# A longer SyncE time for k's turning transfer in the planner of an attention and soft-MoE kernel, with a new order of the attention

## The chip, the cores and the metric

The kernel runs on one core of a Trainium2 chip. The metric is the device time of one execution in microseconds (us). A kernel's time is the median of several executions.

## What is computed

Three layers follow each other. The reference, cut to its core:

```python
# attention: q, k, v are (4, 12, 448, 64)
q_n, k_n = rmsnorm(q, g_q), rmsnorm(k, g_k)
attn = softmax(scale * q_n @ k_n.T)
x = attn @ v                               # -> (1792, 768)
# soft mixture of experts, 8 experts with 4 slots each
logits = x @ phi
slot_input = softmax(logits, axis=0).T @ x
slot_out[e] = relu(slot_input[e] @ w1[e]) @ w2[e]
x = softmax(logits, axis=1) @ slot_out
# one more feed-forward layer
h = x @ w_in
out = (h * sigmoid(1.702 * h)) @ w_out
```

## The kernel before

The attention takes two heads at a time: 24 pairs, numbered p = 0 to 23. Two pairs (four heads) share one load of q, k and v. For each pair the steps are these.

- **Preparation.** `square` and `meansq` (L412, L417), the inverse root (`invert`, L434 to L448), `gain` (L465), `qn` and `kn` (L472). Then q and k are each split into two float16 halves: `qhi` and `khi` on ScalarE (L476, L479), `qlo` (L482) and `klo` (L487). `k2` and `q2` copy the high halves once more (L288 on ScalarE, L290 elsewhere).
- **Turning.** A DMA transpose issued by SyncE (L499) turns the rows so that the head's dimension lies along the partitions: `tka` for k (16 blocks of 128x128), `tqa` for q (8 blocks) and, later, `tqb` for q's second form (8 blocks). Pairs 0 and 1 are turned on TensorE instead. The buffer that `tka` reads exists once (`ka=1`), so `khi` of the next pair has to wait until `tka` has landed.
- **Row maxima.** Four steps `mx` on TensorE (L529) make a first, rough score. Each has a `max` on VectorE (L534). The PSUM tile between them exists once (`mx=1`), so `mx` number g+1 waits for `max` number g. The maxima go into q's second form, which `tqb` turns.
- **Scores.** Seven steps `sc` on TensorE (L545) with seven `exp` on ScalarE (L549), four `pv` steps (L559, L564), partial sums `esum` (L552), the sums' turns, and the output's turn `x` (L610, L611) with its scaling `xmul` (L623, L627).

No order is written out by hand. `op()` records each step with its engine, an estimated duration, a due time and what it needs. `run()` replays them: at each point it takes the engine whose next step can start first, and among the steps of that engine that can start then the one with the smallest due time. The steps are issued in that order, and each engine works through its own row strictly in order. Two tables steer it: `ON` says for each pair which engine does a step (D = VectorE, P = GpSimd, A = ScalarE), and `SHIFT` is added to the due time of each kind of step.

SyncE's row holds all of the attention's loads (`lq`, `lk`, `v`: L386 to L400), the turning transfers, and the first expert weights: `early` (L115, L124) and, near the end, `e0` to `e3` and `ev`, which go into buffers that the attention has given up. A step of SyncE has two prices in the planner. The duration in `op()` is how long SyncE itself is taken, and `QUEUE` says when the transfer will have landed; `QUEUE` counts 3.0 for `tka` and 1.5 for `tqa` and `tqb`.

Where TensorE would stand idle, the planner puts in small matmuls on the identity (`warm`, L380), which compute nothing that is used.

After the attention come the soft-MoE stage (to about 410 us), which streams the expert weights, and the last layer, in which TensorE works without a pause.

Of the kernel before, what the change touches and what calls it, by code (L numbers as in the profile page):

```python
# [20 lines left out]
def soft_moe_block_kernel(  # L21
# [30 lines left out]
    T = 8.862  # L52

    ON = dict(
        gain="PDPDPDDDPDDPDPDPDDPDDDDD",
        qn="DPPDPPPPPPDPPPDPPPPPDPDD",
        kn="DPDDDPPPPPDDPPDPPPDDPDPP",
        qlo="PPDPPPDPDDPPDDPPDPDDPPPD",
        klo="DDDDDDPPPDPDDPDDDPDPDPDD",
        q2="PPDAAADAPDDDDDAAAAPDPPDA",  # L60
        k2="DDDADDADADPDADAAADPAADPA",
        e01="PPDPDPDPPPPPDDDPDDDPDPDP",
        e02="PPDPPPPPPDDDPPPPDDDDDPPD",
        e11="DPPPDDPPPPDDDPDDDDDDPDPP",
        e12="PPDDDPPPPDPDDPPDDDPPDDPD",
        x0="DDDDAAADADDDDAADAADAADDA",
        x1="DAAAADDAADADDADAADDADAAA",
        nr="DPPDPDPPDPDP",
    )
    DEBUG = 0  # L70
    NWARM = 100
# [118 lines left out]
    def new(tag, shape, dt=F32):  # L190
        if tag in rings:
            turns[tag] = turns.get(tag, -1) + 1
            return rings[tag][turns[tag] % BUFS[tag]]
        return pools[tag].tile(shape, dt, tag=tag, name=tag)

    raw, vt, sqt, QA, QAT, KT, QBT = ({} for _ in range(7))
# [14 lines left out]
    def turned(t, at, n):  # L211
        return t[:, at:at + n].bitcast(F16).rearrange("p (a d) -> p a d", d=128)
# [8 lines left out]
    for i, tag in enumerate(("ssq", "y0", "nt")):  # L221
# [4 lines left out]
    qa_t, kk_t = turned(wv_t, 2304, 512), turned(wr_t[1], 2048, 1024)  # L226
# [20 lines left out]
        lq2=(1, 2), lk2=(1, 2), tka=(3.0, 0.8), tqa=(1.5, 0.8), tqb=(1.5, 0.8), lq=(1.2, 2), lk=(1.2, 2), v=(1.2, 2), early=(1.2, 2),  # L247
        ev=(1, 2), e0=(1.3, 2), e1=(1.3, 2), e2=(1, 2), e3=(1, 2),
# [12 lines left out]
    }  # L261

    SHIFT = dict(
        e0=4065.4, e1=1871.6, e2=705.9, e3=1336.9, early=76.2, esum=1946.8, ev=1170.2, exp=938.3, gain=3568,
        guard=-7.4, invert=-243.4, k2=1786.8, khi=-2180.8, klo=-680.2, kn=1837.3, lastlg=-2574.3, lk=1816.2,
        lk2=3100.6, logits=522.6, lq=1423.8, lq2=582.8, max=1121.1, meansq=1101.5, mx=-29, out=798.9,
        pe_tka=-2476.8, pe_tkb=3670.2, pe_tqa=681.5, pe_tqb=-366.9, pv=510.7, q2=1966, qhi=3834, qlo=1235.4,
        qn=1990.6, r_add=3872.4, r_back=3899.1, r_eb=1801, r_exp=-2634.4, r_fade=1302.1, r_gather=624.9,
        r_max=1791.5, r_more=-2250.9, r_neg=1305.5, r_old=1619.3, r_turn=681.3, r_z=352.5, recip=1344.9,
        sc=586, square=-471.5, squarek=473, ssb=-536.7, sumT=1332.9, sums=-8.9, tka=-2650.5, tka0=719.8,  # L270
        tkb=3875.6, tkb0=-229.5, tqa=-2002, tqa0=523.6, tqb=-542.8, tqb0=1302.7, v=4133.3, w_back=1921.6,
        w_copy=1410.9, w_exp=1561, w_guard=-358.8, w_max=-206.5, w_neg=-343.2, w_recip=-2399.9, w_scale=1149.9,
        w_sel=3867.1, w_sum=581.9, w_turn=1912.7, w_z=3874.4, x=2168.9, xmul=1473.5,
    )
    COST = dict(
        gain=(0.6, 1.23), qn=(0.6, 1.02), kn=(0.6, 1.02), qlo=(0.6, 1.12), klo=(0.6, 1.12), q2=(0.2, 1.1, 0.52),
        k2=(0.2, 1.1, 0.52), e01=(0.53, 1.09), e02=(0.53, 1.09), e11=(0.53, 1.09), e12=(0.53, 1.09),
        x0=(0.47, 9, 0.9), x1=(0.47, 9, 0.9), nr=(0.1, 0.3),
# [14 lines left out]
    def op(name, eng, dur, due, fn, needs=(), takes=None, gives=()):  # L293
        names[name] = len(ops)
        due += SHIFT.get(name if isinstance(name, str) else name[0], 0)
        ops.append((name, eng, dur, due, fn, list(needs) + HOLD.get(name, []), takes, list(gives)))
# [200 lines left out]
    def turn(p, tag, store, src):  # L497
        store[p] = new(tag, [128, src.shape[1], P], F16)
        nc.sync.dma_start_transpose(out=store[p], in_=src.rearrange("p a d -> p (a d)"))  # L499

    def pe_turn(tag, src, lo, hi):

        MS[tag] = new("ms", [128, 8, P], F16)
        for a in range(lo, hi):
            nc.tensor.transpose(MS[tag][:, a], src[:, a], ident16)

    def pe_copy(p, tag, store, eng, lo, hi, at=0):
        if p not in store:
            store[p] = new(tag[:3], [128, 16 if tag == "kt" else 8, P], F16)
        copy(eng, store[p][:, at + lo:at + hi], MS[tag if not at else "ka"][:, lo:hi])  # L510
# [148 lines left out]
    for p in range(NP):  # L659
        t = T * p  # L660
        qd = p // 2
        sub = lambda *n: [(x, p) for x in n]
# [35 lines left out]
        op(("k2", p), *on("k2", p)[1:], t - 19.5, lambda p=p: k_again(p), sub("khi", "klo"))  # L698
        op(("q2", p), *on("q2", p)[1:], t - 15, lambda p=p: q_again(p), sub("qhi") + old("qb", ("tqb",)), None, [("qa", p)])
        if p >= NPE:  # L700
            op(("tka", p), "SP", 1.32, t - 16.3, lambda p=p: turn(p, "kt", KT, kk_t), sub("klo", "k2"), ("kt", p), [("ka", p)])
            op(("tqa", p), "SP", 1.32, t - 16.2, lambda p=p: turn(p, "qat", QAT, QA[p]), sub("qhi", "qlo"), ("qat", p), [("qa", p)])
        else:
            for nm, tag, store, src, at, needs, takes, gives in (
                ("tkb", "kt", KT, kb_t, 0, sub("khi"), "kt", []),
                ("tqa", "qat", QAT, qa_t, 0, sub("qhi", "qlo"), "qat", [("qa", p)]),
                ("tka", "ka", KT, ka_t, 8, sub("klo", "k2", "tkb"), None, [("ka", p)]),
            ):
                g = [("ms", nm, p)]
                op(("pe_" + nm, p), "PE", 0.48, t - 16, lambda tag=tag, src=src: pe_turn(tag, src, 0, 8), needs, g[0], gives)  # L710
                op((nm + "0", p), "ACT", 0.48, t - 15.9, lambda p=p, tag=tag, store=store, at=at: pe_copy(p, tag, store, nc.scalar, 0, 4, at), [("pe_" + nm, p)], takes and (takes, p), g)
                op((nm, p), "DVE", 0.27, t - 15.8, lambda p=p, tag=tag, store=store, at=at: pe_copy(p, tag, store, nc.vector, 4, 8, at), [(nm + "0", p)], None, g)
# [82 lines left out]
        if p % 2:  # L795
            t = 2 * T * qd + 2 * T
# [162 lines left out]
    for i, f in enumerate(left):  # L959

        p = 1 + (i - NFIRST) * (NP - 3) // (len(left) - NFIRST)
# [16 lines left out]
    with tc.manual_schedule():  # L978
# [474 lines left out]
        for w in work:  # L1453
            f, n = w[2], w[1]
            x = n / 384
# [75 lines left out]
```

## Time and profile before

| | |
|---|---|
| median of 3 runs | 690.77 us (690.19 to 692.08) |
| the profiled execution | 688.41 us |
| its span, first to last instruction | 686.6 us |
| busy in the span: TensorE, VectorE, ScalarE, GpSimd | 617.3, 396.3, 364.3, 164.5 us |
| TensorE's mean granted clock | 0.974 of full speed |

The busy times are of the whole span. They say little of the stage that is changed, the attention, which takes the first 296 us. Matmuls overlap in the engine and their ends are modelled, so TensorE's busy time is not its time at its peak. Each row of a trace view starts with what it stands for; times are in us unless ns is said.

### The profile page before, as it was taken

Reading aid. Unit: us, or ns where it says so; the run is one execution under the profiler, and the core shown is the slowest. Engines: PE = TensorE matmul, PEld = TensorE weight load, DVE = VectorE, ACT = ScalarE, POOL = GpSimd, SP = SyncE. Lnnn points to the kernel's source line nnn. Section 1 sums busy time; section 2 is a strip of 40 time slices with the busy share of each in tenths; the row PEclk is TensorE's granted clock in tenths of the full one; section 3 lists DMA queues with packets and bytes.
Section 4 is the critical chain, followed back from the end, with each engine's and each line's share of the span. In section 5 each row is a group of like instructions: output and inputs, shape, how many; then the busy total and the mean of one; then the engine's idle time right before and its main releaser. Section 6 shows DMA issues by size and latency. Waiting matters only on the chain.

```text
span 686.6 us, 10997 instructions
## 1 busy us (share of the span) xinstructions
PE 617.3 (90%) x4104; PEld 414.0 (60%) x4104; DVE 396.3 (58%) x657; ACT 364.3 (53%) x756; POOL 164.5 (24%) x193
## 2 busy tenths in 40 slices
PE   2989998999999999986743999999999999999997
PEld 1434343344444343453421344999899999999997
DVE  5978988898899997354444514899401211211211
ACT  4757787769768675643334412897413323432432
POOL 4565775873562551300000200000000000000000
PEclk9999999999999999999876999999999999999999
DMA  8989999998999999689899994761100100100101
GB/s 215 289 162 209 194 198 206 183 181 184 194 185 190 210 227 214 209 321 353 322 407 405 406 349 178 266 232 72 70 1 0 70 1 1 70 0 1 70 1 46
DMA packets 150965, 121.73 MB, mean 177 GB/s; under 512 B 106848, under 2 KB 131680, under 8 KB 150912
## 3 DMA queue, kind: packets, MB, share of 16 engines
q1 hardware_dynamic: 147824, 110.91, 59.7%
q10 hardware_dynamic: 3024, 10.03, 3.8%
q8 instruction: 32, 0.52, 0.3%
q14 instruction: 21, 0.17, 0.1%
q0 software_dynamic: 64, 0.10, 0.1%
HBM read 92.18 MB, written 5.51 MB: 142 GB/s over the span
## 4 chain that ended last, share of the span: by engine, by line
PE 67%; DMA 12%; DVE 11%; ACT 4%; issue 3%; POOL 3%; SPq 1%; ACTq 0%; DVEq 0%; POOLq 0%
PE y L1351 27%; PE y L1368 7%; PE sc L545 6%; PE pv L564 4%; PE so_ps L1154 4%; DVE wr L534 3%; DMA wr<-wr 3%; PE mx L529 2%; DMA wr<-in_q_dram 2%; PE h L1121 2%; PE f L1310 2%; DMA wr<-in_moe_w_dram 2%; DVE wr L417 1%; PE t L1113 1%; PE pv L559 1%
## 5 line engine op out<-in xcount | busy, mean ns | idle before, releaser
L1332 DVE TENSOR_TENSOR gl<-gg,gh 128x384 fp32r<-128x384 f32 (+1 forms) x80 | 42.2, 530 | 154.0 <-ACT gh L1327 153.2
L534 DVE TENSOR_REDUCE wr<-mx 128x2 f16<-128x896 f32 x92 | 99.8, 1085 | 16.1 <-PE mx L529 16.0
L1318 ACT ACTIVATE gg<-f 128x384 f32<-128x384 f32 (+1 forms) x78 | 36.4, 468 | 116.8 <-PE f L1310 115.4
L1351 PE MATMUL y<-wo,gh 128*128 128x384 f32 x352 | 75.3, 335 | 0.0
L549 ACT ACTIVATE e<-sc,esc 128x448 f32<-128x448 f32 x96 | 58.0, 642 | 12.2 <-PE sc L545 8.8
L1351 PEld LDWEIGHTS y<-wo,gh 128*128 128x128 f32 x352 | 62.1, 188 | 0.0
L552 POOL TENSOR_TENSOR es<-es,e 128x448 f32<-128x448 f32 x36 | 44.1, 1236 | 50.6 <-PE pv L564 31.6
L545 PE MATMUL sc<-wr 128*128 128x448 f16 (+1 forms) x192 | 49.0, 365 | 2.2 <-DMA wr<-wr 1.7
L1327 ACT ACTIVATE gh<-gg 128x384 fp32r<-128x384 f32 (+1 forms) x78 | 39.3, 504 | 16.3 <-PE y L1351 10.7
L1351 PE MATMUL y<-wh,gl 128*128 128x384 f32 x176 | 46.8, 337 | 0.0
L1351 PE MATMUL y<-wh,gh 128*128 128x384 f32 x176 | 46.7, 336 | 0.0
L1351 PE MATMUL y<-wl,gh 128*128 128x384 f32 x176 | 46.7, 336 | 0.0
L549 ACT ACTIVATE es<-sc,esc 128x448 f32<-128x448 f32 x54 | 33.5, 642 | 21.6 <-PE sc L545 21.4
L1351 PE MATMUL y<-wo,gl 128*128 128x384 f32 x176 | 44.8, 335 | 0.0
L412 ACT ACTIVATE wr<-wr 128x512 f32<-128x512 f32 x48 | 30.6, 644 | 15.8 <-DMA wr<-in_k_dram 4.8
L472 POOL TENSOR_TENSOR wr<-wr 128x512 f32<-128x512 f32 x31 | 34.6, 1134 | 11.6 <-DVE wr L448 7.8
L545 PEld LDWEIGHTS <-wr 128*128 128x128 f16 (+1 forms) x256 | 19.0, 103 | 30.1 <-issue 21.3
L147 ACT ACTIVATE wi<-wst 128x512 f32<-128x512 f32 x24 | 16.2, 674 | 36.5 <-DMA wr<-in_moe_w_dram 16.1
L144 DVE SCALAR_TENSOR_TENSOR wst<-wst 128x512 uint32<-128x512 uint32 x24 | 16.6, 690 | 29.2 <-ACT wst L150 27.3
L1351 PEld LDWEIGHTS y<-wl,gh 128*128 128x128 f32 x176 | 32.0, 188 | 0.0
L1351 PEld LDWEIGHTS y<-wh,gl 128*128 128x128 f32 x176 | 32.0, 188 | 0.0
L1351 PEld LDWEIGHTS y<-wo,gl 128*128 128x128 f32 x176 | 31.9, 188 | 0.0
(264 smaller groups left out, 1324.6 us busy)
## 6 DMA issues: line engine op xcount, KB each, us to landing
wr<-in_moe_w_dram SPq DMA_DIRECT2D x30, 512.0 KB, 8.8
wt<-in_moe_w_dram SPq DMA_DIRECT2D x24, 512.0 KB, 7.8
wr<-in_moe_w_out_dram SPq DMA_DIRECT2D x15, 768.0 KB, 4.3
wst<-in_moe_w_in_dram ACTq DMA_DIRECT2D x19, 512.0 KB, 6.9
wt<-in_moe_w_dram SPq DMA_DIRECT2D x20, 384.0 KB, 7.8
wr<-in_moe_w_dram SPq DMA_DIRECT2D x20, 384.0 KB, 5.7
out_dram<-o SPq DMA_DIRECT2D x13, 384.0 KB, 2.3
wr<-in_k_dram SPq DMA_DIRECT2D x11, 384.0 KB, 5.1
```

Source lines behind the costliest of these rows:

```text
L412: nc.scalar.activation(out=sqt[p][:, 8 * i:8 * i + 8], in_=rows(p, i), func=AF.Square, scale=D ** -0.5)
L472: eng.tensor_tensor(out=n, in0=n, in1=r.to_broadcast([P, 8, D]), op=ALU.mult)
L534: nc.vector.tensor_reduce(out=lanes(of(qb_t, p), 1)[:m, h:h + n, c, 0:1], in_=MX.pop((p, g))[:m, :n, :S], axis=AX.X, op=ALU.max,)
L545: nc.tensor.matmul(out, cols(a, n, c), cols(b, n), start=first, stop=not first)
L549: nc.scalar.activation(out=E[p, h, c], in_=SC.pop((p, h, c)), func=AF.Exp, scale=esc)
L552: on(f"e{h}{c}", p)[0].tensor_tensor(out=E[p, h, 0], in0=E[p, h, 0], in1=E[p, h, c], op=ALU.add)
L564: nc.tensor.matmul(PV[p][h * D:(h + 1) * D, :], t[:, 6 * n + 3 * h + c], E[p, h, c], start=(c == 0), stop=False)
L1318: nc.scalar.activation(out=ggt[w][:, :w[1]], in_=src[:, :w[1]], func=AF.Silu, scale=1.702)
L1327: nc.scalar.activation(out=gh[:, :w[1]], in_=ggt[w][:, :w[1]], func=AF.Copy)
L1332: nc.vector.tensor_tensor(out=G[w][1][:, :n], in0=ggt[w][:, :n], in1=G[w][0][:, :n].bitcast(F32), op=ALU.subtract)
L1351: nc.tensor.matmul(Y[t, u][:, :384], a[:, ts], b[f][:, u * 384:(u + 1) * 384], start=(f == 0 and i == 0), stop=(f == KF - 1 and i == 2),)
L1368: nc.tensor.matmul(Y[t, u][:, :384], a[:, t * 128:(t + 1) * 128], b[:, u * 384:(u + 1) * 384], start=(f == 0 and j == 0), stop=(f == KF - ...
```

## The change

One number of the planner changes: the time for which SyncE is taken by `tka` goes from 1.32 to 2.9. The two tables `ON` and `SHIFT` are replaced with others. No step is added or removed, and the computation stays the same.

```diff
-        gain="PDPDPDDDPDDPDPDPDDPDDDDD",
+        gain="DDPDDDDDPDDDDDDDDPDDDDPD",
...
-        k2="DDDADDADADPDADAAADPAADPA",
+        k2="DDDADPADAAPAAPAAADADPAPP",
...
-        tkb=3875.6, tkb0=-229.5, tqa=-2002, tqa0=523.6, tqb=-542.8, tqb0=1302.7, v=4133.3, w_back=1921.6,
...
+        tka=-1529.3, tka0=-837.6, tkb=-576.3, tkb0=-287.8, tqa=-219.8, tqa0=-1129.9, tqb=-583.6, tqb0=-981.4,
...
-            op(("tka", p), "SP", 1.32, t - 16.3, lambda p=p: turn(p, "kt", KT, kk_t), sub("klo", "k2"), ("kt", p), [("ka", p)])
+            op(("tka", p), "SP", 2.9, t - 16.3, lambda p=p: turn(p, "kt", KT, kk_t), sub("klo", "k2"), ("kt", p), [("ka", p)])
```

How many of the steps of a kind change engine, by the table `ON` (24 of each kind):

| step | VectorE before, after | GpSimd before, after | ScalarE before, after |
|---|---|---|---|
| `gain` | 16, 20 | 8, 4 | |
| `qn` and `kn` together | 17, 22 | 31, 26 | |
| `qlo` | 10, 12 | 14, 12 | |
| `klo` | 16, 12 | 8, 12 | |
| `q2` and `k2` together | 20, 13 | 9, 11 | 19, 24 |
| the four `esum` together | 46, 40 | 50, 56 | |
| `x0` and `x1` (`xmul`) | 23, 25 | | 25, 23 |

The small steps of `invert` go to GpSimd for three more groups of pairs. The changed file has one line more in `SHIFT`, so that a line behind it has a number higher by one.

The order changes at the following places, among others. First SyncE's row in the middle of the attention, from the turning of k for pair 11 on. Before (`kt` is k's turned tile, 16 blocks; then `qat`, q's; then the loads of q and k for a later group; the fourth row from below is `tqb` of pair 10, the last two are `tqa` and `tka` of pair 12):

```order
L499 DMA_TRANSPOSE kt_159<-wr 128x16x128
L499 DMA_TRANSPOSE qat_151<-wr 128x8x128
L397 DMA wr<-in_q_dram 128x4x192
L400 DMA wr<-in_q_dram 64x4x64
L397 DMA wr<-in_k_dram 128x4x192
L400 DMA wr<-in_k_dram 64x4x64
L499 DMA_TRANSPOSE wr<-wr 128x8x128
L115 DMA wi<-in_moe_w_dram 128x1024
L499 DMA_TRANSPOSE wr<-wr 128x8x128
L499 DMA_TRANSPOSE wr<-wr 128x16x128
```

The same place after:

```order
L500 DMA_TRANSPOSE kt_159<-wr 128x16x128
L500 DMA_TRANSPOSE qat_151<-wr 128x8x128
L500 DMA_TRANSPOSE wr<-wr 128x8x128
L115 DMA wi<-in_moe_w_dram 128x1024
L398 DMA wr<-in_q_dram 128x4x192
L401 DMA wr<-in_q_dram 64x4x64
L398 DMA wr<-in_k_dram 128x4x192
L401 DMA wr<-in_k_dram 64x4x64
L500 DMA_TRANSPOSE wr<-wr 128x16x128
L500 DMA_TRANSPOSE wr<-wr 128x8x128
```

`tqb` of pair 10 now stands ahead of the four loads, and `tka` of pair 12 ahead of its `tqa`. At pairs 6, 12 and 18 the load of k likewise goes behind `tqb`.

Second, SyncE's row near the end, where the weights for freed buffers begin. Before, `tka` of pair 21 is the first row, `tqa` of that pair the second, and the three loads of `e0` (L115) follow:

```order
L499 DMA_TRANSPOSE wr<-wr 128x16x128
L499 DMA_TRANSPOSE wr<-wr 128x8x128
L115 DMA wr<-in_moe_w_dram 128x1024 x3
L499 DMA_TRANSPOSE wr<-wr 128x8x128
L124 DMA wi<-in_moe_w_dram 128x768
```

After:

```order
L115 DMA wr<-in_moe_w_dram 128x1024
L500 DMA_TRANSPOSE wr<-wr 128x8x128
L115 DMA wr<-in_moe_w_dram 128x1024 x2
L500 DMA_TRANSPOSE wr<-wr 128x16x128
L500 DMA_TRANSPOSE wr<-wr 128x8x128
L124 DMA wi<-in_moe_w_dram 128x768
```

All three weight loads now stand ahead of `tka` of pair 21. From `tka` of pair 22 on, SyncE's row is the same but for one weight load that moves ahead of `tqa` of pair 23.

Third, VectorE's row from the last `max` of pair 6 (the 64x2 one) to the last of pair 7. Before:

```order
L534 TENSOR_REDUCE wr<-mx 64x2
L534 TENSOR_REDUCE wr<-mx 128x2
L627 TENSOR_TENSOR xl<-ms,rs 128x4x96
L552 TENSOR_TENSOR wr<-wr,e 128x448
L534 TENSOR_REDUCE wr<-mx 128x2
L465 TENSOR_TENSOR wr<-wr 128x512
L482 TENSOR_TENSOR wr<-wr 128x2x4x64
L417 TENSOR_REDUCE wr<-wr 128x16
L534 TENSOR_REDUCE wr<-mx 128x2
L534 TENSOR_REDUCE wr<-mx 64x2
```

After:

```order
L535 TENSOR_REDUCE wr<-mx 64x2
L628 TENSOR_TENSOR xl<-ms,rs 128x4x96
L473 TENSOR_TENSOR wr<-wr 128x512
L535 TENSOR_REDUCE wr<-mx 128x2 x2
L483 TENSOR_TENSOR wr<-wr 128x2x4x64
L553 TENSOR_TENSOR es_158<-es_158,e 128x448
L535 TENSOR_REDUCE wr<-mx 128x2
L466 TENSOR_TENSOR wr<-wr 128x512
L628 TENSOR_TENSOR xl<-ms,rs 128x4x96
L535 TENSOR_REDUCE wr<-mx 64x2
```

The first two `max` of pair 7 stand next to each other now; between the second and the third there are two steps where there were three.

## Rows read from the trace of the kernel before

**Rows 1.** Busy time by stretch: PE, PEld, DVE, ACT, POOL, granted clock, DMA, GB/s.

```profile
20.00:50.00 30.00, 26.70 (x135) 11.80 (x133) 26.61 (x41) 18.08 (x36) 17.22 (x23) 1.00 0.84 208
50.00:260.00 210.00, 202.31 (x1160) 84.54 (x1158) 190.71 (x281) 159.31 (x356) 123.88 (x121) 1.00 0.97 196
...
296.00:410.00 114.00, 80.10 (x872) 38.63 (x875) 50.73 (x111) 41.62 (x85) 4.50 (x19) 0.87 1.00 377
```

**Rows 2.** Waits of PE, 20 to 50 us: total, times, longest.

```profile
PE mx L529 <- DVE wr L534: 2.4, 4, 1.1
```

**Rows 3.** Waits of PE, 50 to 260 us.

```profile
PE mx L529 <- DVE wr L534: 5.0, 8, 1.2
```

**Rows 4.** Waits of PE, 260 to 296 us.

```profile
PE sc L545 <- DMA wr<-wr: 1.4, 1, 1.4
PE mx L529 <- DMA kt<-wr: 1.2, 1, 1.2
```

**Rows 5.** The chain that ended last: start, us, what.

```profile
42.24 1.63 PE ms L380 x10
...
64.55 1.24 PE sc L545 x6
...
260.70 8.25 DMA kt<-wr
...
270.30 5.82 DMA wr<-wr
```

**Rows 6.** Line L380 from 20 to 296 us: ns min/median/max, first and last start.

```profile
L380 PE MATMUL ms<-ident x33: 269/270/283, 36.0 to 193.6; 128*128 128x256 f16 x33
```

**Rows 7.** Line L499, SyncE: ns min/median/max, first and last start.

```profile
L499 SPq DMA_TRANSPOSE kt<-wr x8: 1317/3104/4851, 29.9 to 260.7; - x8
```

**Rows 8.** DMA issues: median us from issue to landing.

```profile
kt<-wr SPq DMA_TRANSPOSE x8, 5.9
```

**Rows 9.** SyncE's timeline: start, us, what.

```profile
129.74 0.86 SPq L397 DMA_DIRECT2D wr<-in_q_dram  x1
...
133.00 1.28 SPq L499 DMA_TRANSPOSE wr<-wr  x1
...
236.04 3.84 SPq L499 DMA_TRANSPOSE wr<-wr  x2
239.94 2.58 SPq L115 DMA_DIRECT2D wr<-in_moe_w_dram  x3
```

**Rows 10.** ACT's timeline: `khi` of pair 22.

```profile
245.19 0.74 ACT L479 ACTIVATE wr<-wr 128x512 f16<-128x512 f32 x1
```

**Rows 11.** Groups of instructions, 0 to 300 us: busy us, mean ns, idle before.

```profile
L552 POOL TENSOR_TENSOR es<-es,e 128x448 f32<-128x448 f32 x36 | 44.1, 1236 | 50.6 <-PE pv L564 31.6 <-ACT e L549 16.0 <-ACT ssb L581 2.1
L552 DVE TENSOR_TENSOR es<-es,e 128x448 f32<-128x448 f32 x36 | 25.8, 730 | 3.7 <-ACT e L549 2.4 <-PE pv L564 1.3
L472 DVE TENSOR_TENSOR wr<-wr 128x512 f32<-128x512 f32 x17 | 12.8, 773 | 0.0
L465 DVE TENSOR_TENSOR wr<-wr 128x512 f32<-128x512 f32 x16 | 12.5, 780 | 1.4 <-ACT wr L412 1.4
L487 DVE TENSOR_TENSOR wr<-wr 128x512 f16<-128x512 f32 x16 | 11.1, 696 | 0.0
L290 DVE COPY wr<-wr 128x512 f16<-128x512 f16 x20 | 6.6, 330 | 0.0
```

**Rows 12.** Timeline of POOL and DVE around 92 us.

```profile
91.50 2.62 POOL L552 TENSOR_TENSOR es<-es,e 128x448 f32<-128x448 f32 x2 [1.15 <-PE pv L564]
91.56 1.56 DVE L552 TENSOR_TENSOR wr<-wr,e 128x448 f32<-128x448 f32 x1 [0.17 <-PE pv L564]
```

**Rows 13.** PE's timeline at its largest waits for a `max`: start, us, what, [wait].

```profile
94.18 0.36 PE L529 MATMUL mx<-wr 64*128 64x448 f16 x2 [0.81 <-DVE wr L534]
...
109.71 0.38 PE L529 MATMUL mx<-kt,qat 64*64 64x448 f16 x2 [1.18 <-DVE wr L534]
...
227.58 0.36 PE L529 MATMUL mx<-wr 64*128 64x448 f16 x2 [1.01 <-DVE wr L534]
```

More of the change, by code (lines that the diff above doesn't have):

```diff
@@ L54, in soft_moe_block_kernel @@
     ON = dict(
-        gain="PDPDPDDDPDDPDPDPDDPDDDDD",
[L56 to L60, printed above, removed]
-        k2="DDDADDADADPDADAAADPAADPA",
[L62 to L68, printed above, removed]
+        gain="DDPDDDDDPDDDDDDDDPDDDDPD",
+        qn="DPPPPPPDDPPDPDDDPPPPDDPP",
+        kn="DPPDPPPDPPPDPDDDPDDDDDPD",
+        qlo="PPDPPDDPDDPDPDPPDPPDDDDP",
+        klo="DDDDPPPPPPPDDDPDDPPDPDPD",
+        q2="APAAAAAAADPAAPPDADDDADPA",
+        k2="DDDADPADAAPAAPAAADADPAPP",
+        e01="PPDPPPDPPDPPDPDDDPDPDDDP",
+        e02="PPDPDDPPPPDPPPPPDPPDPDPD",
+        e11="DPPPPPDPPDPPDPPDDDPDPPPD",
+        e12="PPDDPPDDPDDPDPPDPPDDPPDD",
+        x0="DDDAAADAADDDDADDADAADDDA",
+        x1="DAADADADDDADDAADDAADAAAA",
+        nr="DPPPPDPPPPPP",
     )
@@ L263, in soft_moe_block_kernel @@
     SHIFT = dict(
[L264 to L270, printed above, removed]
-        tkb=3875.6, tkb0=-229.5, tqa=-2002, tqa0=523.6, tqb=-542.8, tqb0=1302.7, v=4133.3, w_back=1921.6,
-        w_copy=1410.9, w_exp=1561, w_guard=-358.8, w_max=-206.5, w_neg=-343.2, w_recip=-2399.9, w_scale=1149.9,
-        w_sel=3867.1, w_sum=581.9, w_turn=1912.7, w_z=3874.4, x=2168.9, xmul=1473.5,
+        e0=50.1, e1=-652.8, e2=-52.6, e3=-752.8, early=-1419, esum=885.5, ev=761, exp=630.4, gain=3345.6,
+        guard=2335.6, invert=-973.2, k2=740.7, khi=-1227.2, klo=-1190.9, kn=3318.5, lastlg=2716.8, lk=21,
+        lk2=-590.7, logits=-1444.9, lq=-163.4, lq2=-1275.1, max=-652.9, meansq=-556.9, mx=-1056, out=-329.1,
+        pe_tka=-579.6, pe_tkb=1463.7, pe_tqa=1489.8, pe_tqb=-1455.5, pv=-480.7, q2=1791.9, qhi=3283.5,
+        qlo=407.3, qn=4566.8, r_add=-217.5, r_back=455.3, r_eb=93, r_exp=1136.1, r_fade=2451.1,
+        r_gather=-303.2, r_max=2643, r_more=-596.1, r_neg=-961, r_old=422.3, r_turn=718.9, r_z=-1207,
+        recip=-754.3, sc=-66.7, square=344.3, squarek=-646.7, ssb=-969.8, sumT=1085.7, sums=-893.2,
+        tka=-1529.3, tka0=-837.6, tkb=-576.3, tkb0=-287.8, tqa=-219.8, tqa0=-1129.9, tqb=-583.6, tqb0=-981.4,
+        v=399.4, w_back=3031.2, w_copy=2694.9, w_exp=-1075.3, w_guard=-797.8, w_max=-549.4, w_neg=-691.3,
+        w_recip=-21.2, w_scale=-1322.8, w_sel=-307.7, w_sum=427.2, w_turn=221.7, w_z=-843.1, x=1860.8,
+        xmul=3212,
     )
```

## The prediction, made before the run

> **What bounds the kernel now.** I looked first at the busy time by stretch, since only the attention (up to 296 us) changes. From 50 to 260 us TensorE is busy for 202.31 of 210 us at a granted clock of 1.00, VectorE for 190.71 [rows 1]. Busy TensorE time can hide idle time, so I asked the chain of waits how fast the matmuls follow each other: six `sc` matmuls take 1.24 us, 0.207 us each [rows 5], which leaves no visible room between matmuls of 448 columns. In the middle TensorE therefore issues almost without a pause, and what an order can give back is what TensorE stands idle. The waits of TensorE name it. In the head it waits 2.4 us for row maxima [rows 2], in the middle 5.0 us in eight waits for them [rows 3], and in the tail 1.2 us for k's turned tile and 1.4 us for the second form of q [rows 4]. To that come 33 filler matmuls [rows 6] at 1.63/10 = 0.163 us [rows 5], 5.4 us, most of them in the head. The sum is 2.4 + 5.0 + 2.6 + 5.4 = 15.4 us. **No order of the attention can gain more than about that**, and much of the head is the latency of the first loads and maxima.
>
> Behind the attention the DMA engines are at a share of 1.00 from 296 to 410 us [rows 1], and their large loads start when the attention gives up its memory. So I pass a shift of the attention's end on to the kernel's end one for one.
>
> **The change, part by part.**
>
> *SyncE's price.* The planner counted 1.32 us of SyncE for each `tka`; the trace has a median of 3.104 us and a range of 1.317 to 4.851 [rows 7]. With 22 such turns (pairs 2 to 23) it missed 22 x (3.10 - 1.32) = 39 us of SyncE's time; with 2.9 it misses 22 x 0.2 = 4.5 us. The old plan saw SyncE free earlier than it was, and put loads of later pairs ahead of a `tqb` on which the next scores wait. In the middle of SyncE's row the four load instructions ahead of `tqb` of pair 10 start at 129.74 and the `tqb` at 133.00 [rows 9]: 3.3 us that the new row saves this transfer. Pairs 6, 12 and 18 save about half of it, as only k's load goes behind. On TensorE little of this shows: the middle has no large wait for a turned tile, because `pv`, `x` and `sums` of other pairs fill in. Bounds: 0, and 1.0 us (about a third of one such saving); I take **-0.5 us**, the middle. What is late next is VectorE's maxima.
>
> *VectorE's work.* By the counts of the table and the means of [rows 11], VectorE gets four more `gain` (4 x 0.780 = 3.1) and five more `qn` or `kn` (5 x 0.773 = 3.9), and loses six `esum` (6 x 0.730 = 4.4), four `klo` (4 x 0.696 = 2.8) and seven copies (7 x 0.330 = 2.3): 7.0 - 9.5 = -2.5 us. Two more `qlo` and two more `xmul` at up to 0.78 (+3.1 at most) and twelve small steps of `invert` that leave (-4.0 at most, priced as the copies) I take to cancel. GpSimd gets twelve large steps and gives up eleven, so that its load grows by about one of 1.236 us and the small steps. A saving of 2.5 us on an engine that is busy for 190.71 of 210 us is small by itself; what matters is where the work stands.
>
> *Where it stands.* Three of the eight middle waits hold 0.81 + 1.18 + 1.01 = 3.0 of the 5.0 us [rows 13]. The first follows an `esum` between the first two `max` of pair 7, which took 1.56 us [rows 12]; in the new row these `max` are neighbours. The second follows two `kn` that stand ahead of the third `max` of pair 8; in the new row they come elsewhere. The third follows `xmul` and two `esum` ahead of the second `max` of pair 19; there, too, the new row has less. But the same steps must go somewhere, and other `max` now have two `esum` or a `klo` and two reductions ahead of them. Bounds: all three waits vanish and nothing comes (-3.0), or as much comes as goes (0, or above if the new places are worse). I take a third of the 5.0 us, **-1.7 us**.
>
> That `esum` ran beside one of GpSimd's, which started 0.06 us earlier [rows 12]; its excess over the mean of 0.730 [rows 11] is 0.83 us, and the wait of 0.81 follows. The Trainium skill (SBUF — State Buffer, Who interferes with whom) says that such a VectorE step with two inputs and a GpSimd step exclude each other for a whole instruction; this row agrees. By that rule the nine `gain`, `qn` and `kn` that come to VectorE would be as exposed as what leaves, the saving in this paragraph would be 0, and the sum -0.9 us.
>
> *The head.* Between the first `max` of pair 0 and the last of pair 1 VectorE loses two `kn` or `qn`, a `gain` and a copy, and gets one `gain`: -0.77 - 0.77 - 0.78 - 0.33 + 0.78 = -1.9 us [rows 11]. The transfer that decides there, `tqb` of pair 1, still stands behind `tka` of pair 3 on SyncE, and the fillers stay about as many. Bounds -1.0 and +1.0; I take **-0.4 us**.
>
> *The tail.* `tka` of pair 23 takes 8.25 us to land at 260.70, against a median of 5.9 [rows 5, 8], with three weight loads ahead of it; `tqb` of pair 22, queued on SyncE behind a load that waits for that landing, takes 5.82 us at 270.30 [rows 5]. The new row keeps this order. So the 2.6 us stay: **0**, with bounds of -2.6 (if pair 23 is prepared earlier) and, above, what rival B tells.
>
> Sum: -0.5 - 1.7 - 0.4 + 0 = -2.6 us. The profiled execution took 688.41 us for a span of 686.6, so it would go to 685.8. The median of the runs before lies 2.36 us above the profiled execution; I carry that over: 690.77 - 2.6 = **688.2 us**. A change under 0.3% (2.1 us) is about what a measurement of this kernel can't tell from none.
>
> **The rivals.**
>
> *A: the idle time only moves.* TensorE is nearly full, VectorE too, and a new order makes as many waits as it removes. For it: the waits are short and scattered, and the tail, where the DMA waits are, stays in its order. Against it: three known places are lighter. Time: between the sum without the saving at the maxima, 690.77 - 0.9 = 689.9, and 690.8.
>
> *B: weight loads ahead of k's turn, slower.* All three loads of `e0` now stand ahead of `tka` of pair 21. They take SyncE 2.58 us [rows 9], and a turn behind three loads landed 8.25 - 5.9 = 2.35 us later than the median [rows 5, 8]: 4.9 us in all. k's buffer exists once, so pairs 22 and 23 follow in a ring: `khi` of pair 22 waits for that landing. The cover: `tka` of pair 21 was issued at 236.04 and would have landed by the median at about 241.9 (an estimate), and `khi` of pair 22 ran at 245.19 [rows 9, 10], 3.3 us later. From 3.3 us of delay on, the ring reaches the tail, which has no other work left. If the steps ahead of `khi` come earlier than before, the cover is gone, and with the gain at the maxima the time is 690.77 + 4.9 - 1.7 = 694.0 us.
>
> *C: the change doesn't do what it says.* 2.9 us is a flat price, but the same transfer took SyncE 1.317 us at one end and 4.851 at the other [rows 7]. If the time depends on what is queued ahead, a plan with 2.9 everywhere is as wrong as one with 1.32, at other places, and the refitted order is merely another order. If waits for maxima grow by half of their 5.0 us, the time is 693.3 us.
>
> **How the numbers follow.** The forecast has a chance of 0.42, A 0.33, B 0.17 and C 0.08. A is the case within 0.3%, B and C are slower: faster 0.42, same 0.33, slower 0.25. The predicted time is the forecast's, 688.2 us. Its own low end takes every lower bound: -3.0 - 1.0 - 1.0 - 2.6 = -7.6, or 683.2 us. The range reaches from there to B's 694.0 us; beyond lie the part of B without any gain and something of C.
>
> **What would show it.** Right: the waits of TensorE for maxima from 50 to 260 us come to about 3.3 us instead of 5.0, with none over 0.8 us at pairs 7, 8 and 19; `tqb` of pair 10 starts within 1 us after its last `max`; TensorE's last matmul of the attention ends some 2.6 us earlier. Wrong by A: those waits again sum to about 5 us, at other pairs. Wrong by B: a wait of TensorE for k's tile of pair 21 or 22, and the third and fourth turns from the end start later against the scores. Wrong by C: `kt` turns that still range from 1.3 to 5 us, and new waits where the plan had SyncE free. The prediction also fails if the soft-MoE stage doesn't follow the attention's end one for one.

## The result, and the profile after

The changed kernel takes **681.44 us** (median of 4, 680.23 to 684.39) against 690.48 us before (median of 4), a ratio of 0.988 with a 95% interval of 0.983 to 0.993. A second measurement on another chip gave 682.1 us against 688.25 us, 0.9915 (0.9888 to 0.9942). So the change saves 6 to 9 us. The forecast was 2.6 us less, 688.2, with a range from 683.2 up: the sign was right, the size too small by more than half, and the first measurement lies below the range.

The profiled execution took 681.2 us for a span of 679.4. TensorE's waits from 20 to 50, 50 to 260 and 260 to 296 us (what it waited for, total, times, longest) answer to [rows 2 to 4]:

```profile
PE mx L530 <- DVE wr L535: 1.2, 2, 0.9
PE sc L530 <- DVE wr L535: 0.5, 1, 0.5
...
PE mx L530 <- DVE wr L535: 1.8, 3, 0.7
PE mx L530 <- DMA qat<-wr: 0.7, 1, 0.7
...
PE sc L546 <- DMA wr<-wr: 2.5, 1, 2.5
PE ms L875 <- DVE macc L822: 0.7, 1, 0.7
```

In the middle 5.0 us of waits for maxima have become 1.8 in this execution, and none is over 0.7. The second profiled execution of the same kernel (`a_again`, below) has 2.7 us of them, since a wait at pair 4 is 1.63 us there and 0.70 here:

```profile
PE mx L530 <- DVE wr L535: 2.7, 3, 1.6
```

In the tail the wait for k's turned tile is gone, that for `tqb` has grown from 1.4 to 2.5 (2.3 in the second). Busy time by stretch, with the columns of [rows 1]:

```profile
50.00:260.00 210.00, 206.64 (x1214) 88.05 (x1212) 193.75 (x272) 165.32 (x361) 129.30 (x138) 1.00 0.99 205
```

TensorE is busy for 206.64 of 210 us where it was 202.31 (204.86 in the second execution), and the stretch holds 54 more matmuls. The table follows the kernels to the end, in us from start to start of instructions in the profiled runs; the first column counts from the span's start. "Soft-MoE" runs from the last matmul of the attention's last `x` to the first `f` of the last layer. The step of the last layer lies between its last `y` matmul of L1368 and the first of L1351 (line numbers of before).

| | last `x` | soft-MoE | step in the last layer | from there to the last `y` |
|---|---|---|---|---|
| before | 296.11 | 138.75 | 2.82 | 192.44 |
| after, first run | 289.12 | 140.27 | 0.52 | 193.02 |
| after, second run (`a_again`) | 290.10 | 140.05 | 0.52 | 193.02 |

The 7.2 us of span are therefore -7.0 in the attention, +1.5 in the soft-MoE stage, and -2.30 + 0.58 = -1.7 in the last layer, where I had expected nothing at all.

### The profile page after: what moved, and what is told of

Same layout as the page of the kernel before. It is cut to its first block, busy times and chain, and to the rows that moved or that the text cites. A ratio compares the mean times of both kernels' runs of the same rounds, so it can differ in the third digit from the quotient of the medians.

```text
span 679.4 us, 11043 instructions
## 1 busy us (share of the span) xinstructions
PE 616.7 (91%) x4109; PEld 415.6 (61%) x4109; DVE 394.0 (58%) x641; ACT 367.0 (54%) x753; POOL 168.6 (25%) x209
## 4 chain that ended last, share of the span: by engine, by line
PE 68%; DVE 13%; DMA 10%; ACT 3%; issue 3%; POOL 1%; SPq 1%; ACTq 0%; DVEq 0%; POOLq 0%
PE y L1352 27%; PE y L1369 7%; PE pv L565 6%; PE sc L546 5%; DVE wr L535 4%; DMA wr<-in_moe_w_dram 3%; DMA wt<-in_moe_w_dram 3%; PE so_ps L1155 3%; PE mx L530 2%; PE h L1122 2%; DMA wr<-in_k_dram 2%; PE pv L560 2%; PE f L1311 2%; PE t L1114 1%; DVE es L553 1%
## 5 line engine op out<-in xcount | busy, mean ns | idle before, releaser
L550 ACT ACTIVATE e<-sc,esc 128x448 f32<-128x448 f32 x96 | 57.4, 636 | 10.5 <-PE sc L546 8.6
L473 POOL TENSOR_TENSOR wr<-wr 128x512 f32<-128x512 f32 x26 | 30.2, 1180 | 11.6 <-DVE wr L466 7.4
L418 DVE TENSOR_REDUCE wr<-wr 128x16 f32<-128x1024 f32 x24 | 29.1, 1211 | 5.6 <-ACT wr L413 5.6
```

The costliest lines, as they stand in the source:

```text
L473: eng.tensor_tensor(out=n, in0=n, in1=r.to_broadcast([P, 8, D]), op=ALU.mult)
L550: nc.scalar.activation(out=E[p, h, c], in_=SC.pop((p, h, c)), func=AF.Exp, scale=esc)
```

## The experiments

"Ratio" is the time against before on the same chip, with its 95% interval; several kernels share a chip and the runs of before on it. "End" is the start of the attention's last `x` matmul (296.1 before).

### The last layer: one name in two plans

The changed table `SHIFT` also reaches the last layer, whose plan has steps named `out` as well (they bring y out of PSUM). `e3_out` gives only these steps the new value in the kernel before, `e4_no_out` takes it away from the changed kernel:

```diff
-        due += SHIFT.get(name if isinstance(name, str) else name[0], 0)
+        due += -329.1 if name[0] == "out" and len(name) == 4 else SHIFT.get(name if isinstance(name, str) else name[0], 0)
```

(`e4_no_out` has 798.9 there.)

> The kernel before, with one thing of the change: in the last layer's plan the step that brings y out of PSUM gets the new shift of its due time (-329.1 instead of +798.9). The attention's order is word for word the one of before. Theory (the table is read by the last layer too, where a step has the same name; the matmuls no longer wait for gg at the end of the first block of rows): the attention ends as before at 296 us, TensorE's two waits for gg near 488 and 489 us (0.71 and 0.32 us) are gone, and the kernel takes 2.0 to 2.5 us less, about 688.3 us beside 690.5. Rival (the shorter last layer of the changed kernel only follows from what came ahead of it): no difference, within 0.5 us of before.

> The kernel after, with one thing undone: in the last layer's plan the step that brings y out of PSUM gets the old shift (+798.9 instead of -329.1). The attention's order is word for word the one of after. Theory: attention and soft-MoE stage as in the kernel after, the waits for gg at the first block's end are back, and the kernel takes 2.0 to 2.5 us more than after, about 683.7 us. Rival: no difference from after, 681.4 us. Together with the run of before with the new shift alone this says whether the two parts simply add up.

`e3_out`: ratio 0.9979 (0.9957 to 1.000), end 296.14. `e4_no_out`: 0.9941 (0.9917 to 0.9964), end 290.59. TensorE's timeline at the step, first of before, then of `e4_no_out` (start, us, what, the wait in brackets):

```profile
488.26 0.82 PE L1310 MATMUL f<-cT,ust 128*128 128x384 f32 x2 [0.71 <-ACT gg L1318]
489.40 0.45 PE L1310 MATMUL f<-cT,ust 128*128 128x384 f32 x1 [0.32 <-ACT gg L1318]
```

```profile
481.80 0.82 PE L1311 MATMUL f<-cT,ust 128*128 128x384 f32 x2 [0.71 <-ACT gg L1319]
482.94 0.45 PE L1311 MATMUL f<-cT,ust 128*128 128x384 f32 x1 [0.32 <-ACT gg L1319]
```

The two waits belong to the old value, whatever the attention does. In all traces of this study the step is 2.81 to 2.82 us with the old value and 0.52 us with the new one, and the rest of the layer is some 0.55 us longer with the new one. So this part is worth **1.7 us** and simply adds. The expected 2.0 to 2.5 missed the 0.55. `e3_out` hides it in its profile, since its soft-MoE stage took 140.34 us, 1.6 more than before with the same order: that stage varies from run to run (137.8 to 143.5 us over all kernels, with no clear relation to where the attention ended). What goes with it is TensorE's granted clock in the stage. Here is the stage in before and in after, with the columns of [rows 1]:

```profile
296.11:434.86 138.75, 102.69 (x1150) 52.87 (x1150) 62.97 (x139) 51.00 (x101) 4.50 (x19) 0.88 0.94 354
289.12:429.39 140.27, 105.65 (x1157) 54.06 (x1156) 62.97 (x139) 51.13 (x101) 4.08 (x19) 0.87 0.93 350
```

The clock is 0.88 in all seven profiled executions that took 137.8 to 138.9 us, and 0.86 or 0.87 in nine of the eleven that took longer (`h1_spA` and `r1_old` have 0.88). Which of the two follows the other isn't shown.

### The price or the tables

`e1_price` changes the price alone, `e2_tables` puts it back in the changed kernel. Each is one line:

```diff
-            op(("tka", p), "SP", 1.32, t - 16.3, lambda p=p: turn(p, "kt", KT, kk_t), sub("klo", "k2"), ("kt", p), [("ka", p)])
+            op(("tka", p), "SP", 2.9, t - 16.3, lambda p=p: turn(p, "kt", KT, kk_t), sub("klo", "k2"), ("kt", p), [("ka", p)])
```

> The kernel before with one number changed: the planner's SyncE time for k's turn is 2.9 instead of 1.32; both tables stay the old ones. The order still changes at more than half of TensorE's places. Theory (the refitted tables hold the gain; the old tables were fitted to the old price): no gain, 689 to 697 us, and TensorE's waits for row maxima from 50 to 260 us stay at 5 us or more. Rival 1 (the longer price alone puts SyncE's transfers where they belong, and that is the gain): 682 to 686 us, with those waits at 3 us or less. The last layer keeps its old order in either case, since its table entry is the old one.

> The kernel after with the planner's SyncE time for k's turn put back from 2.9 to 1.32; both tables stay the new ones. Theory (tables and price were fitted together, and the gain belongs to the one order that they make together): most of the attention's gain is lost, last matmul of the attention at 292 us or later instead of 289.1, in all 684 to 690 us. Rival 1 (the price holds the gain): as before without the last layer's part, 687 to 690 us. Rival 2 (the tables hold it whatever the price, because most of it comes from which engine does a step): the attention ends by 290 us, in all 680 to 683 us.

`e1_price`: 715.78 us, ratio 1.039 (1.035 to 1.044), end 314.98. `e2_tables`: 691.14 us, 1.0043 (1.0021 to 1.0065), end 300.48. The price alone costs far more than my theory had, and the tables alone lose everything. Most of the first was in the plan: with the old tables and the new price the planner lets the last `x` start at 304.3, against 287.0 before. In `e1_price` k's turn of pair 19, whose input was ready at 216.0 (`klo` ends at 215.1, `k2` at 216.0), stands behind a `tqb` and several groups of loads in SyncE's row, and SyncE idles between them:

```profile
215.37 1.23 SPq L499 DMA_TRANSPOSE qbt<-wr  x1
218.32 0.37 SPq L397 DMA_DIRECT2D wr<-in_q_dram  x1
...
222.56 0.38 SPq L386 DMA_DIRECT2D v<-in_v_dram  x1
223.47 1.26 SPq L390 DMA_DIRECT2D v<-in_v_dram  x2
229.33 5.20 SPq L499 DMA_TRANSPOSE wr<-wr  x3
```

The turn, the first of the three in the last row, is issued 13.3 us after its input. The last 4.6 of these are not the queue's: the loads are issued by 224.73, and the turn then waits for its output buffer (`kt=3`), which the last `sc` of pair 16 still reads:

```profile
228.71 0.55 PE L545 MATMUL sc<-wr 128*64 128x448 f16 x4
```

TensorE's clock fell there too, which before it did nowhere in the attention (stretch, then PE, PEld, DVE, ACT, POOL, granted clock, DMA, GB/s; 1.00 is 2.4 GHz, and 0.73 a mix of that level and the one of 1.2):

```profile
200.00:210.00 10.00, 7.51 (x53) 3.42 (x52) 8.99 (x18) 6.08 (x13) 3.13 (x3) 1.00 1.05 202
210.00:220.00 10.00, 7.95 (x35) 3.56 (x36) 9.69 (x16) 6.10 (x14) 4.01 (x5) 0.73 0.61 131
```

### SyncE's row by itself

For these and the following kernels I wrote the rows of all engines out as lists and let the planner only replay them, so that one row or one step can be exchanged while the rest stays word for word:

```diff
             for e, rs in ready.items():
+                if fixed_rows:
+                    rs = [names[todo[e][0]]] if todo[e] and names[todo[e][0]] in rs else []
```

`h1_spA` is before with SyncE's row of after, `h2_spB` the reverse.

> The changed kernel itself, once more, beside the kernels that differ from it in one thing, so that these can be compared with it on one chip. Theory and rival alike: 0.988 of before, some 8 us less. If the ratio comes out above 0.992, part of the first measurement was chance and the parts have to be sized by this one.

> The kernel before, all engines' rows word for word, but SyncE's row in the attention is that of the changed kernel (14 steps or groups stand elsewhere: tqb of pair 10 ahead of four loads, k's loads behind tqb, e0 ahead of k's turn of pair 21, and so on). Tables of before. Theory (the gain is in TensorE's waits for VectorE's maxima; in the trace of after, the turns wait on SyncE for 93.7 us in all, against 97.8 before, which is nothing): the attention ends within 1.5 us of before, the time within 2 us. Rival (the longer price works through SyncE's row): attention 4 to 7 us earlier, kernel about 683 to 686 us on a chip where before takes 690.

> The changed kernel, all engines' rows word for word, but SyncE's row in the attention is that of the kernel before. Theory: within 2 us of the changed kernel; the rest of its order doesn't need the new row of SyncE. Rival: 4 to 7 us are lost, and TensorE waits for turned tiles (tqb of pairs 6, 10, 12, 18).

`h1_spA`: 709.07 us, ratio 1.030 (1.028 to 1.033), end 316.53. `h2_spB`: 692.87 us, 1.0057 (1.0033 to 1.0082), end 300.61. The new row costs 20 us in the old order, where my theory had no change and its rival a gain: both fail. Its absence costs 10.5 us in the new order; there the rival had the way and the place (TensorE waits 6.5 us for turned tiles from 50 to 260 us), but 4 to 7 us. In `h2_spB` k's turn of pair 13, ready at 146.0, stands behind q's turn of that pair, whose input is ready only at 149.9, and behind a load of q. SyncE (the last row is k's turn) and then TensorE:

```profile
145.61 0.58 SPq L115 DMA_DIRECT2D wi<-in_moe_w_dram  x1
150.07 2.07 SPq L655 DMA_TRANSPOSE wr<-wr  x1
152.20 0.57 SPq L553 DMA_DIRECT2D wr<-in_q_dram  x1
152.82 0.63 SPq L556 DMA_DIRECT2D wr<-in_q_dram  x1
153.56 3.50 SPq L655 DMA_TRANSPOSE wr<-wr  x1
```

```profile
159.00 0.36 PE L685 MATMUL mx<-wr 64*128 64x448 f16 x2 [3.23 <-DMA wr<-wr]
```

In after the same turn is issued at 146.9. And `h1_spA` shows the prediction's rival B, which the changed kernel itself doesn't: all of `e0` ahead of k's turn of pair 21, with the rest of the order as it was. The turn's input was ready at 249.7, when `k2` ended (`klo` had ended at 246.5). The first load of `e0` waits for its buffer until 251.7, `tqa` and the other two loads follow, and the turn is issued at 254.66, 4.9 us late (the row also holds `tqb` of pair 20), and lands at 263.2:

```profile
251.73 0.35 SPq L115 DMA_DIRECT2D wr<-in_moe_w_dram  x1
252.17 1.24 SPq L653 DMA_TRANSPOSE wr<-wr  x1
253.46 1.10 SPq L115 DMA_DIRECT2D wr<-in_moe_w_dram  x2
254.66 7.75 SPq L653 DMA_TRANSPOSE wr<-wr  x2
```

```profile
263.35 0.56 PE L683 MATMUL mx<-wr 64*128 64x448 f16 x2 [4.29 <-DMA wr<-wr]
```

The 4.29 us are close to the 4.9 that rival B was priced at, though a part of the delay here is a load's wait for its buffer, which B didn't count. In after its cover holds, since the input is ready at 230.8 and the turn lands at 240.4, as `mx` of pair 21 begins.

Two things have to be kept apart from the row itself. The planner, which replays these rows, already lets the last `x` start at 314.2 in `h1_spA` (287.0 before) and at 300.2 in `h2_spB` (286.2 after), so that losses of this size could be read from the plan. And TensorE's clock falls with the stalls, here in the wait of 4.29 us:

```profile
260.00:270.00 10.00, 6.65 (x24) 2.22 (x24) 5.35 (x5) 2.84 (x10) 4.32 (x4) 0.66 0.54 115
```

In `h1_spA` the mean from 50 us to the attention's end is 0.96, in `e1_price` 0.97, in `h2_spB` and `e2_tables` 0.99, against 1.00 before and after. An estimate for `h1_spA`: 4% of 266 us is some 10 us at most of its 20, if TensorE had work all the time that the clock was low.

### The waits for maxima by themselves

`h3_moves` and `z2_kn11` are before with some VectorE steps put behind a `max`:

```diff
+    MOVES = [  # engine, step, placed right behind this step
+        ('DVE', ('esum', 5, 1, 1), ('max', 7, 3)),
+        ('DVE', ('meansq', 10), ('max', 7, 3)),
+        ('DVE', ('kn', 11), ('max', 8, 2)),
+        ('DVE', ('esum', 17, 1, 1), ('max', 19, 1)),
+    ]
```

`z2_kn11` has the third of these alone.

> The kernel before, all rows word for word, but four steps on VectorE stand behind a max instead of ahead of it: esum of pair 5 and meansq of pair 10 behind the last max of pair 7, kn of pair 11 behind the third max of pair 8, esum of pair 17 behind the second max of pair 19. No table, no price, no other engine changes. Theory (a wait of TensorE for a max is lost time one for one): the waits of 0.81, 0.87, 1.18 and 1.01 us shrink to under 0.4 each, the attention ends 2 to 3.5 us earlier. Rival (idle time only moves: the steps put behind are late for others): attention within 0.7 us of before.

> The kernel before, all rows word for word, but one step: VectorE does kn of pair 11 behind the third max of pair 8 instead of ahead of it. In the planner this costs nothing (287.1 against 287.0). Theory (a wait that nothing else covers is worth its length): TensorE's wait of 1.18 us for that max shrinks to about 0.4, and from pair 9 on everything is 0.7 to 0.8 us earlier. Rival (idle only moves): the next wait, for xmul, grows, and pair 9 ends as before, within 0.3 us.

`h3_moves`: 692.16 us, ratio 1.0054 (1.0034 to 1.0073), end 297.42, slower than before. Its TensorE:

```profile
101.17 1.39 PE L737 MATMUL ms<-wr,ones 128*32 128x448 f32 x2 [3.23 <-POOL wr L717]
112.93 0.38 PE L694 MATMUL mx<-kt,qat 64*64 64x448 f16 x2 [0.36 <-DVE wr L699]
```

The waits of pair 7 are gone and that of pair 8 fell from 1.18 to 0.36. But the `esum` that was put behind feeds one of GpSimd's, and that one the `sums`, which stands next in TensorE's row: 3.23 us there for 0.81 + 0.87 saved. The wait at a `max` was only where the lateness showed. `z2_kn11`, the one move that I tried by itself: the wait is 0.58, pair 9 ends 0.6 us earlier, and no wait in the middle grows in return; by pair 23 it is 2.0 us, end 294.10. The 1.4 us beyond the 0.6 come behind pair 15, where nothing was moved; two executions of the old order (before and `e3_out`) differ by up to 1.0 us at a pair. Its ratio, 0.9987 (0.9966 to 1.0009), can't be told from none. So in one trace an uncovered wait was worth about what it lost, as my theory had it; the time doesn't show it, and whether the other large waits can be had as freely wasn't tried one by one.

### Is the new price needed? Refits of my own

A random search over both tables for the shortest plan, from the tables of before, twice with the old price (`r1_old`, `r2_old`) and twice with the new one (`r3_new`, `r4_new`). All have the new `out` in the last layer.

> A refit of my own, with the OLD price: tables ON and SHIFT found by a random search (300,000 trial plans from the tables of before) for the shortest planned order of the attention, SyncE's time for k's turn at 1.32. The planner lets the last matmuls of the attention start at 280.5 us (before: planned 287.0, ran 296.1; changed kernel: planned 286.2, ran 289.1 to 290.1). The last layer's out shift is the new one. Theory A (the longer price makes the plan hold on the chip: 2.9 runs 3 to 4 us behind its plan, 1.32 runs 9 us behind): the attention ends 9 to 11 us behind the plan, near 290 us, as the changed kernel. Theory B (the price is indifferent; a refit as such gives what the chip gives, and the distance to the plan is chance from order to order): no difference in that distance between the two refits with 1.32 and the two with 2.9; each 3 to 10 us.

> A second refit with the OLD price 1.32, from another start of the random search. Planned start of the attention's last matmuls: 282.6 us. Theory A: ends 9 to 11 us behind the plan, near 292.5 us, kernel about 684 us. Theory B: 3 to 10 us behind, no worse as a group than the two refits with 2.9.

> The same search with the NEW price 2.9, from the same tables of before (which with this price are planned to 304.3 us). Planned start of the attention's last matmuls after the search: 282.6 us, so as long as the second refit with 1.32. Theory A: 3 to 4 us behind the plan, near 286 us, kernel about 677 us. Theory B: as the refits with 1.32.

> A second refit with the NEW price 2.9, from another start of the search; planned 282.6 us. Theory A: near 286 us, kernel about 677 us, and TensorE waits less for turned tiles (DMA) than in the refits with 1.32. Theory B: as the refits with 1.32, 3 to 10 us behind the plan.

The planner is part of the kernel, so its plan is known when the kernel is built. Its start of the last `x` step against that of the last `x` matmul on the chip:

| | price | plan | chip | behind | time, ratio |
|---|---|---|---|---|---|
| before | 1.32 | 287.0 | 296.1 | 9.1 | |
| after, two runs | 2.9 | 286.2 | 289.1, 290.1 | 2.9, 3.9 | 0.988, 0.9915 |
| `r1_old` | 1.32 | 280.5 | 293.9 | 13.4 | 687.22, 0.9969 (0.9948 to 0.9989) |
| `r2_old` | 1.32 | 282.6 | 296.5 | 13.9 | 688.51, 0.9994 (0.9974 to 1.0014) |
| `r3_new` | 2.9 | 282.6 | 300.0 | 17.4 | 691.49, 1.0035 (1.0013 to 1.0056) |
| `r4_new` | 2.9 | 282.6 | 294.6 | 12.0 | 684.79, 0.9943 (0.9917 to 0.9968) |

Theory A, that the new price makes the plan hold, falls: the two prices lie alike, 12 to 17 us behind. `e1_price`, with the new price, is 10.7 us behind its 304.3. (Theory B's 3 to 10 us were too few.) The planner gives the changed order 0.85 us over the old one; the chip gives it 6 to 7. In `r3_new` VectorE's two-input steps take longer, by its lines and then those of after, 50 to 280 us (busy us, mean ns):

```profile
L553 DVE TENSOR_TENSOR es<-es,e 128x448 f32<-128x448 f32 x26 | 21.7, 845 | 0.1
L473 DVE TENSOR_TENSOR wr<-wr 128x512 f32<-128x512 f32 x16 | 16.1, 1013 | 0.0
```

```profile
L553 DVE TENSOR_TENSOR es<-es,e 128x448 f32<-128x448 f32 x32 | 23.8, 753 | 2.3 <-PE pv L565 1.9 <-ACT e L550 0.2
L473 DVE TENSOR_TENSOR wr<-wr 128x512 f32<-128x512 f32 x19 | 16.5, 887 | 0.0
```

That may be a part of why `r3_new` falls behind, but it doesn't set the refits apart: in `r4_new`, 12.0 us behind, the same steps take 0.736 and 0.890 us, as in after. Nor does it tell why after keeps its plan, for between before and after these steps differ little (0.732 and 0.753 us for the `esum` on `es`).

### Halves joined, and the tail

`s1_AB` has the changed order up to the last `exp` of pair 12 and the old one behind it, `s2_BA` the reverse.

> The order of the changed kernel up to the last exp of pair 12, behind it the remaining steps in the order of before (rows written out; each step on the engine that its own half's table gives). The last layer as before. Theory (the gain consists of separate pieces along the order, and what is won is kept): the attention is 3.5 to 4.5 us earlier at pair 12 and stays so, ends near 292.5 us, against 296.1 before and 290 after. Rival (only a whole order that was fitted in one piece is good; at the seam engines' rows don't match): what was won by pair 12 is lost again at the seam, end at 296 us or later.

> The other way round: the order of before up to the last exp of pair 12, then that of the changed kernel. Theory: as before up to pair 12, then 2 to 3 us won in the second half and the tail, end near 293.5 us. Rival: lost at the seam, end at 296 us or later.

`s1_AB`: ratio 1.0002 (0.9991 to 1.0013), end 296.60; 3.8 us ahead at pair 12, all lost by pair 13. `s2_BA`: 1.0008 (0.9992 to 1.0024), end 298.00. The rival holds. In `s1_AB` the largest piece of the loss is one wait for a `max` just behind the seam:

```profile
174.07 0.36 PE L683 MATMUL mx<-kt,qat 64*128 64x448 f16 x2 [2.54 <-DVE wr L688]
```

`f_tail` is the changed kernel with four weight loads put behind two turns in SyncE's row:

```diff
+        ('SP', ('ev', 3), ('tka', 23)),
+        ('SP', ('e1', 2), ('tqb', 22)),
+        ('SP', ('ev', 0), ('e1', 2)),
+        ('SP', ('ev', 1), ('ev', 0)),
```

> The changed kernel, all rows word for word, but four weight loads (the last ev, the last e1, two ev) stand behind tka of pair 23 and tqb of pair 22 in SyncE's row instead of ahead of them. In the changed kernel tqb of pair 22 is issued 4.5 us after its last max, queued behind a load that waits for the landing of tka of pair 23, and TensorE waits 2.3 to 2.7 us for it. Theory (lost time on the path): that wait falls under 0.5 us, the attention ends about 2 us earlier, the kernel takes 1 to 2 us less than the changed one, if the later weights are not missed by the experts. Rival (the next thing is late): the wait is replaced by one for a maximum or for tqb of pair 23, gain below 0.7 us.

`f_tail`: **679.4 us**, ratio 0.9853 (0.9829 to 0.9877), end 288.31. SyncE in after, then in `f_tail`:

```profile
256.33 3.43 SPq L500 DMA_TRANSPOSE kt<-wr  x1
261.78 0.33 SPq L115 DMA_DIRECT2D wr<-in_moe_w_dram  x1
262.17 0.90 SPq L124 DMA_DIRECT2D wr<-in_moe_w_dram  x2
263.17 1.23 SPq L500 DMA_TRANSPOSE wr<-wr  x1
```

```profile
255.67 4.32 SPq L666 DMA_TRANSPOSE kt<-wr  x1
260.16 0.46 SPq L124 DMA_DIRECT2D wr<-in_moe_w_dram  x1
260.67 2.37 SPq L666 DMA_TRANSPOSE wr<-wr  x1
```

`tqb` of pair 22 no longer stands behind a load that waits for the turn ahead of it, and TensorE's 2.5 us wait is gone from its list. From pair 20 to pair 23 `f_tail` wins 3.0 us on before, where the three runs with the changed attention win 0.1 to 0.5. Of the kernels here it is the shortest. Its interval lies just under that of `a_again`, on another chip, and overlaps that of the first measurement of after (0.983 to 0.993), so that its lead of some 2 us over after is shown by the trace better than by the time.

## Why the prediction was too small, by its own steps

The sum failed at three terms. The maxima were mis-sized: -1.7 us, where their waits fell by 3.2 and 2.3 us in the two executions. The time between matmuls that stand in no list of waits was put at nothing, because TensorE "issues almost without a pause"; it fell by 2.7 and 3.4 us. And the last layer had no term at all; it gave 1.7 us. What made the second of these fall isn't known.

**The maxima: right in kind, too small.** I took a third of 5.0 us. The waits fell by 3.2 us in the first execution and 2.3 in the second; none is over 0.8 at pairs 7, 8 or 19. What is left stands at pairs 4, 7 and 9: 0.70, 0.65 and 0.43 us, in the second 1.63, 0.66 and 0.43. The wait at pair 4 is new there, as rival A has it. The reason that I gave for a third was that the steps must go somewhere. In the changed order they found places that cost little; `h3_moves` shows one move that didn't, so the caution was sound and the value wrong. That the steps which came to VectorE are exposed beside GpSimd, as the Trainium skill (SBUF — State Buffer, Who interferes with whom) has it, agrees with the rows: from 0 to 300 us `qn` and `kn` now take 0.859 us on the mean, against 0.773 [rows 11]. Those that ran beside no GpSimd step took 0.67 us on the mean before and after, none over 0.69; beside one (6 of 17 before, 11 of 22 after) up to 1.54. But the saving at the maxima was not eaten up by that.

**The sum left out the pace of the matmuls.** I read "almost without a pause" from six matmuls. From the first `mx` to the last `x` the attention became 8.3 us shorter (276.43 to 268.11; it starts 1.3 us later), of which the listed waits hold 5.6 (13.03 to 7.45). In the second execution it became 6.4 us shorter (270.01), of which the waits hold 3.0 (10.00). The rest, 2.7 and 3.4 us, is in shorter intervals from one matmul's start to the next that no list of waits shows: behind an `sc` matmul 193 ns before and 189 after, 384 of them, 1.5 us; behind a matmul of L564 216 and 213, 288 of them, 0.8 us. The profile counts these as busy time: pauses too short for the list come to 0.6 us before and after. The sum had no term for this, and why the pace changed isn't shown.

**SyncE: the transfers as foreseen, the value not.** `tqb` of pair 10 starts at 130.76, 0.1 us after its last `max`, ahead of the loads:

```profile
130.76 1.34 SPq L500 DMA_TRANSPOSE wr<-wr  x1
132.15 0.57 SPq L115 DMA_DIRECT2D wi<-in_moe_w_dram  x1
132.78 0.44 SPq L398 DMA_DIRECT2D wr<-in_q_dram  x1
```

I priced that at -0.5 us, with a bound of -1.0, because TensorE had no large wait for turned tiles in the old order. That costs the row with all other rows standing still. `h1_spA` and `h2_spB` show that there is no such number for the row alone: the same exchange is +20 us or -10.5 us, by the rows around it.

**The head and the tail** came out as forecast: pairs 1 to 4 end within 1.2 us of before, either way, and the tail's waits are 2.5 us where I had 2.6 stay. That they stayed was right and that they could be had for four moved loads was overlooked.

**The last layer was missed.** I took the tables to concern the attention alone. That a shift is looked up by name, and that `out` is a name of both plans, was to be read in `op()`. It is 1.7 of the 6 to 9 us.

**One for one holds only roughly.** The soft-MoE stage took 1.5 us longer behind the earlier attention (1.3 in the second execution), at a clock of 0.87 instead of 0.88; in after's chain it is DMA that ends last there:

```profile
301.98 7.67 DMA wt<-in_moe_w_dram
309.71 5.50 DMA wt<-in_moe_w_dram
```

But it did so in `e3_out` without an earlier attention, and in `e4_no_out` it was 0.9 us shorter than before. A shift of the attention goes through, give or take 1.5 us.

**The rivals.** A (the idle only moves) is what happens to most of the other orders tried here, but not to this one. B's mechanism is real and has its price, as `h1_spA` shows; its cover was there. C (a flat price is wrong) is right about the price and not about the time: SyncE's time for the 22 turns of k still ranges from 1.317 to 4.944 us in after. (The 1.317 to 4.851 that I gave for before are of the eight turns of [rows 7]; all 22 have 1.317 to 5.046, with the same median.) The order that these tables make needs the price (`e2_tables`, without it, ends 10 to 11 us later), but the refits show no gain from the price as such.

**What stays open.** Why the changed order runs only 3 to 4 us behind its plan and that of before 9 isn't settled. The lead grows at pairs 5 to 8 (2.6 us), 9 to 12 (2.0 to 2.4) and 13 to 20 (2.1 to 2.4), but the joined halves show that it can't be taken apart at a seam, and no single cause was isolated beyond the waits named above. Nor is it shown that the price had a part in finding this order; the refits only show that it isn't enough. The two new tables weren't tried apart, so whether the choice of engines (`ON`) or the due times (`SHIFT`) carry the gain is open too.

## What to carry to other kernels

When a planner's tables change, look up every place that reads them by name before saying which stage is touched. Don't price one engine's row with the others standing still: exchange it in a replay of the fixed rows if its worth matters, and look whether a wait that is moved away comes back at whoever needs the step that was put behind. A shorter plan is no forecast once it was searched for; four plans that were 4.4 to 6.5 us shorter than the old one ended their attention from 2.2 us earlier to 3.9 us later.

## What the runs showed of the hardware beyond that

SyncE's time for one 16-block turn isn't a constant of the transfer. Over all 22 of them (those of [rows 7] and 14 that are written to tiles named `wr`) it ranges from 1.317 to 5.046 us in before, median 3.10, and from 1.317 to 4.944 in after, median 3.00, with the same transfers in another company. TensorE's granted clock, 1.00 through the attention before and after, fell to 0.73 from 210 to 220 us in `e1_price`, behind 10 us in which it was busy for 7.51; in the tail of after it was busy for 7.50 of 10 us from 260 to 270 and kept 1.00.
